# Batches in every eighth row of a quadrant, in a decode block of attention and MLP on one core

## The chip, the core and the metric

The kernel runs on one core of a Trainium2 chip. A core has a matrix engine (TensorE, PE in the profile; its weight loads are listed apart as PEld), a vector engine (VectorE, DVE), a scalar engine (ScalarE, ACT), GpSimd (POOL) and SyncE (SP), which here only issues DMAs. The engines run beside each other and wait for one another on semaphores. Sixteen DMA engines move data between the chip's memory (HBM) and the core's on-chip memory (SBUF, 128 partitions); TensorE writes into a second one (PSUM, 128 partitions). Compute engines read both, DMAs here only HBM and SBUF.

The metric is the time of one execution on the device, in microseconds (us). The kernel before takes 214.59 us, the median of three runs (214.48 to 214.62).

## The reference

One decode step for a batch of four tokens. `x` has 448 numbers per token; there are 16 query heads on 8 key and value heads, of 256 numbers each. Attention sees the last 1024 of 4096 cached positions. Everything is float32.

```python
h  = x + attention(layernorm(x), k_cache, v_cache, wq, wo)     # window W = 1024
y  = layernorm(layernorm(h))
h2 = h + gelu(y @ w1 + b1) @ w2 + b2                           # 448 -> 1792 -> 448
```

The caches dominate: per key/value head, 4 batches x 1024 positions x 256 numbers for the keys and as much for the values, read once.

## The kernel before, in words

**Quadrants.** A matmul with few output rows uses only a part of the matrix engine. The kernel therefore gives each group of 32 output partitions (a quadrant) a matmul of its own, four beside each other. In the attention one quadrant is one batch. From the attention's output projection on, one quadrant `j` holds one quarter of the columns, and the four batches are rows `32 j + 0, 1, 2, 3` of it: the first four rows of each quadrant. The other 28 rows hold zeros or are not used. `Q` is 32, `B` is 4, `P` is 128, `H` is 64, `D` is 448, `F` is 1792, `FQ` is 448 (a quarter of `F`).

**Loads.** All large loads are issued by SP in program order through `load` (line 52): `wq0`, then `k0`, two small pieces `wq1_last` (line 73), and then keys and values of the heads in turn (`k1`, `v0`, `k2`, `v1`, ...), some 5 MB each, with the projection's weights packed behind them. Keys and values have a ring of two buffers each. The last loads are the values of head 7 in four pieces, `w1` in two and `w2` in three (8, 4 and 2 of its 14 chunks). The framework gives the DMAs, SP's and ACT's in one count, eight semaphores in turn; a DMA that gets a semaphore again first waits for the one that had it before.

**The small rows.** `rs` (lines 129 to 133) is a tile of 128 x 704: a quarter of `x`, of `b2` and of `b1` for each quadrant, in its first four rows. POOL clears it, then ACT issues four DMAs, one for a quadrant, each of 4 rows of 2816 bytes. It is read first on line 358, when the attention is done.

**The heads.** Each head's round projects the next queries, makes scores (line 182), softmax, transposes (207), values (219), normalises (236), transposes the output (240) and copies it into `oT` (lines 243 and 244): a tile of 128 x 4 x 32, cleared once at the start, of whose 32 columns the first four are written. `add_output` (248) multiplies it with `wo` into `acc`; its stationary operand is the whole 32 columns, so that a quadrant's other 28 rows come out zero. The last head's product (line 335) goes straight into four quadrants, 112 or 128 columns each.

**The end of the kernel.** Line 358 adds `x` and sums; two row means over the quadrants (line 349) centre the rows; `pz` (373) turns the rows into columns with `rows_of`, the columns of the identity that stand for the batches, as the moving operand; line 374 copies them into `zT`. Line 388 multiplies `zT` with `w1`, four chunks by four quadrants, into `pu`: the first chunk with 32 stationary columns, the other three with the 4 that hold batches. Line 401 scales and adds `b1`, 402 is gelu, lines 407 and 409 transpose with `rows_of` into `put`, lines 411 (DVE) and 414 (ACT) copy into `gT`. Line 421 multiplies the first 8 chunks of `gT` with `w2` into `pa` (chunks 0 to 3 with 32 columns, 4 to 7 with 4), ACT copies `pa` to `pas` (425). Line 431 multiplies chunks 8 to 13 into `py`, the first of them with 32 columns and the others with 4; after chunk 9 line 256 adds `pas`. Line 437 adds `hb` (residual and `b2`) into `res`, and line 438 stores `res`, all 128 partitions of 128 numbers. The host picks the first four rows of each quadrant.

The order of TensorE's work is the program's, written out by hand, with a few idle matmuls (`keep_warm`, line 308) between; the other engines' order is set by the framework's scheduler.

Of the kernel before, what the change touches and what calls it, by code (L numbers as in the profile page):

```python
# [8 lines left out]
F32 = mybir.dt.float32  # L9
# [6 lines left out]
B, D = 4, 448  # L16
HQ, HKV, SK, DH = 16, 8, 4096, 256
REP = HQ // HKV
W = min(4096, max(256, SK // 4))
F = 1792  # L20
P = 128
H = P // 2
ND = 4
NKC = W // P
NFC = F // P
FQ = F // 4
Q = 32
CACHE = NKC * B * DH
WEIGHTS = 4 * D
EPS = 1e-5  # L30
# [3 lines left out]
def block_kernel(ctx: ExitStack, tc, rows, wq0, k0, wq1, kq, vo, w1, w2, out):  # L34
    nc = tc.nc
# [12 lines left out]
    def load(kind, src, pieces, name):  # L48
        t = ring.tile([P, CACHE + WEIGHTS], F32, tag=kind, name=name)
        at = 0  # L50
        for n in pieces:
            nc.sync.dma_start(t[:, at : at + n], src[:, at : at + n])  # L52
            at += n
        return t


    def wq_parts(t, last=None):
        parts = [(a, yT[:, a, :], slice(0, 512), t[:, a * 512 : (a + 1) * 512]) for a in range(3)]
        if last is not None:
            return parts + [(3, yT[:H, 3, :], slice(0, 512), last)]  # L60
        for i in range(2):
            parts.append((3, yT[:, 3 + i, :], slice(i * 2 * P, (i + 1) * 2 * P), t[:, 3 * 512 :]))
        return parts


    def load_k(g):
        half = CACHE // 2
        if g == 0:
            t = load("k", k0, (CACHE + 3 * 512,), "k0")


            for i in range(2):
                nc.sync.dma_start(
                    wq1_last[i * Q : (i + 1) * Q, :], wq1[i].rearrange("e (p c) -> e p c", c=512)[:, :4, :]
                )
            last = wq1_last
        else:
            pieces = (CACHE + WEIGHTS,) if g + 1 < HKV else (CACHE,)
            t = load("k", kq[g - 1], pieces, f"k{g}")
            last = None  # L80
        kt = [t[:, i * half : (i + 1) * half].rearrange("p (c b k) -> p c b k", c=2, b=B) for i in range(2)]
        return kt, wq_parts(t[:, CACHE:], last) if g + 1 < HKV else None


    def load_v(g):
        pieces = (CACHE + WEIGHTS,)
        if g == HKV - 1:
            pieces = (CACHE // 4, CACHE // 2, CACHE // 4, WEIGHTS)
        t = load("v", vo[g], pieces, f"v{g}")
        v = t[:, :CACHE].rearrange("p (c b d) -> p c b d", c=NKC, b=B)  # L90
        return [v[:, c : c + 2] for c in range(0, NKC, 2)], t[:, CACHE:].rearrange("p (j e) -> p j e", j=4)


    ident = const.tile([P, P], F32, name="ident")
# [5 lines left out]

    sel = const.tile([P, Q], F32, name="sel")
    nc.vector.tensor_add(sel, ident[:, 0:Q], ident[:, Q : 2 * Q])
    nc.vector.tensor_add(sel, sel, ident[:, 2 * Q : 3 * Q])
    nc.vector.tensor_add(sel, sel, ident[:, 3 * Q : 4 * Q])


    yT = const.tile([P, ND + 1, Q], F32, name="yT")
    nc.vector.memset(yT, 0.0)
    wq1_last = const.tile([H, 512], F32, name="wq1_last")
    zT = const.tile([P, ND, Q], F32, name="zT")  # L110
# [5 lines left out]
        nc.vector.tensor_scalar_mul(fold[: 3 * Q, j, :], sel[: 3 * Q, :], 1.0 / D)  # L116
        nc.vector.tensor_scalar_mul(fold[3 * Q :, j, :], sel[3 * Q :, :], 0.5 / D)
    fold = fold.rearrange("p j q -> p (j q)")
    rows_of = ident.rearrange("p (j q) -> p j q", j=4)[:, :, :B]
    qT = [const.tile([P, 2, B, Q], F32, name=f"qT{i}") for i in range(2)]  # L120
    pT = [const.tile([P, NKC // 2, B, Q], F32, name=f"pT{i}") for i in range(2)]
    oT = [const.tile([P, 4, Q], F32, name=f"oT{i}") for i in range(2)]
    gT = const.tile([P, NFC, Q], F32, name="gT")
# [4 lines left out]

    rs = const.tile([P, 2 * P + FQ], F32, name="rs")
    nc.gpsimd.memset(rs, 0.0)  # L130
    for j in range(4):
        nc.scalar.dma_start(rs[j * Q : j * Q + B, :], rows[j])
    xb, b2b, b1b = rs[:, :P], rs[:, P : 2 * P], rs[:, 2 * P :]


# [14 lines left out]
    def rsqrt(dst, var, name):  # L150
        ve = work.tile(list(dst.shape), F32, tag="ve", name=f"ve_{name}")
        nc.vector.tensor_scalar_add(ve, var, EPS)  # L152
        nc.gpsimd.tensor_tensor(dst, ve, mhalf[: dst.shape[0], : dst.shape[1]], op=ALU.pow)  # L153
# [74 lines left out]
    def columns(t, j):  # L228
        if j < 3:
            return t[:, j * P : (j + 1) * P].rearrange("p (i c) -> p i c", i=2)  # L230
        return t[:, None, 3 * P :].to_broadcast([t.shape[0], 2, H])


    def transposed_output(g, po, rec):
        o = work.tile([P, 2, DH], F32, tag="o", name=f"o{g}")
        nc.vector.tensor_scalar_mul(o, po, rec)  # L236
        pt = ps_m.tile([P, 2, 2, P], F32, tag="m", name=f"pot{g}")
        for i in range(2):
            for c in range(2):
                nc.tensor.transpose(pt[:, i, c], o[:, i, c * P : (c + 1) * P], ident)  # L240
        dst = oT[g % 2].rearrange("p (r c) q -> p c r q", r=REP)[:, :, :, :B]
        src = pt.rearrange("p i c (b q) -> p i c q b", b=B)
        nc.vector.tensor_copy(dst, src[:, 0, :, :REP])  # L243
        nc.vector.tensor_add(dst, dst, src[:, 1, :, REP : 2 * REP])  # L244
# [9 lines left out]
    def add_quadrants(dst, t, start):  # L254
        for j in range(4):
            nc.tensor.matmul(dst[j * Q : (j + 1) * Q], sel, columns(t, j), start=start, stop=False)  # L256
# [20 lines left out]
    p, rec = scores(0, kt)  # L277
    project_q(1, wqt)
    transpose_p(0, p)
    for g in range(HKV - 2):  # L280
        kt, wqt = load_k(g + 1)
        vt, wot = load_v(g)
        p, rec_next = scores(g + 1, kt)
# [9 lines left out]
    g = HKV - 2  # L293
# [6 lines left out]
    w2t = [t[:, c * D : (c + 1) * D] for c in range(NFC)]  # L300
    p, rec_last = scores(g + 1, kt)
# [4 lines left out]
    def keep_warm(n, warm):  # L306
        for _ in range(n):
            nc.tensor.matmul(warm[:Q], idle[:, :Q], idle, start=True, stop=True)  # L308
# [24 lines left out]
    for i in range(4):  # L333
        for j in range(4):
            nc.tensor.matmul(
                ph[j * Q : (j + 1) * Q], oT[(g + 1) % 2][:, i, :], columns(wo_last[:, i, :], j),
                start=False, stop=(i == 3),
# [3 lines left out]
    def w1_part(a, j):  # L341
        if a < 3:
            return slice(0, P), w1t[a][:, FQ * j : FQ * (j + 1)]
        rows = slice(H * (j // 2), H * (j // 2) + H)
        return rows, w1t[a][rows, FQ * (j % 2) : FQ * (j % 2 + 1)]


    def row_mean(sums, at, name):
        nc.tensor.matmul(at, fold, sums, start=True, stop=True)
        return at  # L350

    def stat(name):
        return once.tile([P, 1], F32, tag=name, name=name)
# [6 lines left out]
    m = row_mean(hs, pm[:, 0:1], "m")  # L360
# [4 lines left out]
    m = row_mean(ds, pm2[:, 0:1], "m2")  # L365
# [5 lines left out]
    nc.scalar.activation(junk, z, AF.Square, accum_out=zv)  # L371
    pz = ps_m.tile([P, 4, B], F32, tag="m", name="pz")
    nc.tensor.matmul(pz, z, rows_of, start=True, stop=True)
    nc.vector.tensor_copy(zT[:, :, :B], pz)
    hb = once.tile([P, P], F32, tag="hb", name="hb")
    nc.vector.tensor_add(hb, h, b2b)
    keep_warm(1, warm)
# [4 lines left out]
    pu = ps_s.tile([P, 512], F32, tag="s", name="pu")[:, :FQ]  # L382
    pv = ps_m.tile([P, 2], F32, tag="m", name="pv")
    for a in range(ND):
        m = Q if a == 0 else B
        for j in range(4):
            rows, w = w1_part(a, j)
            nc.tensor.matmul(
                pu[j * Q : j * Q + m, :], zT[rows, a, :m], w, start=(a == 0), stop=(a == ND - 1),
            )  # L390
        if a == 0:
            rsqrt(r1, row_mean(dv, pv[:, 0:1], "v1"), "r1")
        if a == 1:
            v2 = stat("v2")
            nc.vector.tensor_scalar(v2, row_mean(zv, pv[:, 1:2], "v2"), r1, r1, op0=ALU.mult, op1=ALU.mult)
            rsqrt(s, v2, "r2")
            nc.vector.tensor_mul(s, s, r1)
# [7 lines left out]
    put = ps_m.tile([P, 4, 4, B], F32, tag="m", name="put")  # L405
# [2 lines left out]
    for rows in (slice(0, H), slice(H, P)):  # L408
        nc.tensor.matmul(put[rows, 3], u[:, 3 * P :], rows_of, start=True, stop=True)
    dst = gT[:, :12, :].rearrange("p (c j) q -> p c j q", c=3)  # L410
    nc.vector.tensor_copy(dst[:, :, :, :B], put[:, :3])

    for i, rows in enumerate((slice(0, H), slice(H, P))):
        nc.scalar.copy(gT[rows, 12:, :B], put[rows, 3].rearrange("p (j i) q -> p j i q", i=2)[:, :, i, :])
    keep_warm(1, warm)

    first = 8
    pa = ps_w.tile([P, D], F32, tag="acc", name="pa")
    for c in range(first):
        j, m = c % 4, Q if c < 4 else B  # L420
        nc.tensor.matmul(
            pa[j * Q : j * Q + m, :], gT[:, c, :m], w2t[c], start=(c < 4), stop=(c >= first - 4),
        )
    pas = once.tile([P, D], F32, tag="u", name="pas")
    nc.scalar.copy(pas, pa)
    py = ps_o.tile([P, 2, H], F32, tag="o", name="py")
    for c in range(first, NFC):
        for j in range(4):
            m, n = (Q, 2) if c == first else (B, 2 if j < 3 else 1)
            w = columns(w2t[c], j) if n == 2 else w2t[c][:, None, 3 * P :]  # L430
            nc.tensor.matmul(  # L431
                py[j * Q : j * Q + m, :n, :], gT[:, c, :m], w, start=(c == first), stop=(c == NFC - 1),
            )
        if c == first + 1:
            add_quadrants(py, pas, False)
    res = once.tile([P, P], F32, tag="res", name="res")
    nc.vector.tensor_add(res, py.rearrange("p i c -> p (i c)"), hb)  # L437
    nc.sync.dma_start(out, res)


# [64 lines left out]
```

## Time and profile before

| | before |
|---|---|
| median of 3 runs | 214.59 us (214.48 to 214.62) |
| profiled execution, from first to last instruction (span) | 212.9 us |
| TensorE busy | 137.9 us (65%) |
| VectorE busy | 39.2 us (18%) |
| ScalarE busy | 21.0 us (10%) |
| GpSimd busy | 5.6 us (3%) |
| DMA moved | 88.46 MB, 415 GB/s over the span |
| mean granted TensorE clock | 0.872 |

The profile is of one execution and prints no other time of it than its span; the runs above are others. The median of the runs is 1.7 us above the span. Busy time is an instruction's own time; waits are not in it. The page's second part cuts the span into 40 slices, its fourth follows the chain of work that ended last back from the last instruction. Matmuls of float32 appear twice in the lists, since each runs in two passes.

### The profile page before, as it was taken

What the parts mean: (1) busy time and instruction counts of PE and PEld (TensorE: products, weight loads), DVE (VectorE), ACT (ScalarE), POOL (GpSimd) and SP (SyncE); (2) the same over time, 40 slices, a digit from 0 to 9 for tenths busy, and PEclk for the clock granted to TensorE, in tenths of its full rate; (3) what the DMA queues carried; (4) which work ended last, traced back from release to release, by engine and by line L of the source; (5) the groups of instructions that cost most, each with busy time, mean ns of one, the idle gap of its engine ahead of it and who ended that gap; (6) DMA issues with size and microseconds to landing.
All of it is one profiled execution on the core that took longest, in us unless ns stands there. A gap on an engine that the chain in (4) does not pass through costs nothing.

```text
span 212.9 us, 2306 instructions
## 1 busy us (share of the span) xinstructions
PE 137.9 (65%) x971; PEld 49.1 (23%) x971; DVE 39.2 (18%) x167; ACT 21.0 (10%) x52; POOL 5.6 (3%) x17
## 2 busy tenths in 40 slices
PE   0456868093886739583986348382948476798994
PEld 0322233021231212211231113120222123234432
DVE  1420324001130202210130104110230231022320
ACT  0210213000030000300030003000030001000311
POOL 6100000000000000000000000000000000000110
PEclk9999999669597966969599859979797999699999
DMA  7999998999989999999999999999989999999991
GB/s 291 426 399 469 398 465 378 459 465 390 458 378 465 465 390 458 398 446 465 390 458 405 443 465 386 465 413 428 461 375 468 440 428 390 417 418 433 424 390 60
DMA packets 3865, 88.46 MB, mean 415 GB/s; under 512 B 448, under 2 KB 576, under 8 KB 1168
## 3 DMA queue, kind: packets, MB, share of 16 engines
q1 hardware_dynamic: 3824, 88.29, 96.9%
q8 instruction: 7, 0.11, 0.2%
q10 hardware_dynamic: 32, 0.05, 0.1%
q14 instruction: 2, 0.02, 0.0%
HBM read 88.26 MB, written 0.07 MB: 415 GB/s over the span
## 4 chain that ended last, share of the span: by engine, by line
DMA 85%; PE 11%; DVE 2%; issue 0%; SPq 0%
DMA v<-vo 65%; DMA w<-w 12%; DMA k<-k 8%; PE po L219 8%; PE acc L248 1%; DVE o L236 1%; PE pot L240 1%; PE py L431 1%; DVE oT L243 0%; DVE oT L244 0%; SPq L52 0%; DVE res L437 0%; PE py L256 0%
## 5 line engine op out<-in xcount | busy, mean ns | idle before, releaser
L182 PE MATMUL s<-k,qT 128*32 128x512 f32 x256 | 42.3, 822 | 24.7 <-DMA k<-kq 22.6
L219 PE MATMUL po<-v,pT 128*32 128x512 f32 x256 | 40.0, 772 | 19.6 <-DMA v<-vo 19.6
L186 DVE TENSOR_REDUCE mx<-s 128x1 f32<-128x512 f32 x16 | 11.1, 691 | 67.4 <-PE s L182 67.4
L182 PEld LDWEIGHTS s<-k,qT 128*32 128x32 f32 x256 | 10.0, 146 | 54.7 <-issue 29.4
L219 PEld LDWEIGHTS po<-v,pT 128*32 128x32 f32 x256 | 10.7, 135 | 42.3 <-issue 31.4
L161 ACT COPY qs<-pq 128x512 f32<-128x512 f32 x8 | 4.7, 586 | 135.8 <-PE pq L159 135.8
L236 DVE TENSOR_SCALAR o<-po,rec 128x512 f32<-128x512 f32 x8 | 6.0, 750 | 60.2 <-PE po L219 60.2
L194 ACT ACTIVATE p<-s,nm 128x512 f32<-128x512 f32 x16 | 10.9, 690 | 18.4 <-DVE nm L190 18.4
L207 PE MATMUL ppt<-ident,p 128*128 128x128 f32 x64 | 10.5, 286 | 2.0 <-ACT p L194 1.7
L165 PE MATMUL pqt<-ident,qs 128*128 128x128 f32 x32 | 5.7, 304 | 6.2 <-ACT qs L161 6.2
L240 PE MATMUL pot<-ident,o 128*128 128x128 f32 x32 | 5.2, 286 | 5.7 <-DVE o L236 5.7
L248 PE MATMUL acc<-v,oT 128*32 128x448 f32 x56 | 6.7, 551 | 3.3 <-DVE oT L244 3.3
L207 PEld LDWEIGHTS ppt<-ident,p 128*128 128x128 f32 x64 | 6.7, 140 | 6.0 <-ACT p L194 6.0
L159 PE MATMUL pq<-k,yT 128*32 128x512 f32 (+1 forms) x66 | 7.3, 515 | 0.0
L308 PE MATMUL warm<-idle 128*32 128x512 bf16 x25 | 7.3, 382 | 0.0
L240 PEld LDWEIGHTS pot<-ident,o 128*128 128x128 f32 x32 | 3.3, 140 | 13.0 <-DVE o L236 13.0
L165 PEld LDWEIGHTS pqt<-ident,qs 128*128 128x128 f32 x32 | 3.6, 150 | 10.9 <-ACT qs L161 9.1
L153 POOL TENSOR_TENSOR r<-ve_r,mhalf 128x1 f32<-128x1 f32 x2 | 1.1, 544 | 191.9 <-DVE ve_r L152 191.9
L211 DVE COPY pT<-ppt 128x16 f32<-128x16 f32 x32 | 4.7, 170 | 4.7 <-PE ppt L207 4.7
L159 PEld LDWEIGHTS pq<-k,yT 128*32 128x32 f32 x66 | 3.1, 110 | 6.1 <-issue 4.8
L138 PE MATMUL pm_x<-wq,mean 128*128 128x12 f32 x2 | 0.6, 363 | 5.8 <-DMA wq<-wq 5.8
L167 DVE TENSOR_REDUCE sm<-pqt 128x16 f32<-128x64 f32 x8 | 1.8, 225 | 13.0 <-PE pqt L165 13.0
(101 smaller groups left out, 60.9 us busy)
## 6 DMA issues: line engine op xcount, KB each, us to landing
v<-vo SPq DMA_DIRECT2D x7, 4992.0 KB, 31.8
k<-kq SPq DMA_DIRECT2D x6, 4992.0 KB, 32.0
k<-k SPq DMA_DIRECT2D x1, 4864.0 KB, 16.3
k<-kq SPq DMA_DIRECT2D x1, 4096.0 KB
w<-w SPq DMA_DIRECT2D x2, 1792.0 KB
v<-vo SPq DMA_DIRECT2D x2, 1024.0 KB, 22.2
v<-vo SPq DMA_DIRECT2D x1, 2048.0 KB
w<-w SPq DMA_DIRECT2D x1, 1344.0 KB
```

The lines of the kernel that those rows point to most:

```text
L159: nc.tensor.matmul(pq[j * Q : (j + 1) * Q, cols], y, w, start=True, stop=True)
L161: nc.scalar.copy(qs, pq)
L165: nc.tensor.transpose(pt[:, i, :], qs[:, i * P : (i + 1) * P], ident)
L182: nc.tensor.matmul(s[b * Q : (b + 1) * Q, :], qT[g % 2][:, c, b, :], kt[h][:, c, b, :], start=(c == 0), stop=(c == 1),)
L186: nc.vector.reduce_max(mx[:, h : h + 1], s, axis=AX.X)
L194: nc.scalar.activation(p[:, h * 512 : (h + 1) * 512], halves[h], AF.Exp, bias=nm, scale=SCALE, accum_out=sums[:, h : h + 1],)
L207: nc.tensor.transpose(pt[:, c, :], p[:, (4 * h + c) * P : (4 * h + c + 1) * P], ident)
L219: nc.tensor.matmul(po[b * Q : (b + 1) * Q], pT[g % 2][:, c, b, :], vt[c][:, :, b, :], start=(c == 0), stop=(c == NKC // 2 - 1),)
L236: nc.vector.tensor_scalar_mul(o, po, rec)
L240: nc.tensor.transpose(pt[:, i, c], o[:, i, c * P : (c + 1) * P], ident)
L248: nc.tensor.matmul(acc[i * Q : (i + 1) * Q, :], oT[g % 2][:, i, :], wt[:, i, :], start=(g == 0), stop=(g == HKV - 2),)
L308: nc.tensor.matmul(warm[:Q], idle[:, :Q], idle, start=True, stop=True)
```

## The change

The four batches of a quadrant move from rows 0, 1, 2, 3 to rows 0, 8, 16, 24, from the attention's output on. All sixteen rows of a tile are then one pattern, every eighth of the 128 partitions. With it:

- `rows_of` takes every eighth column of the identity; `oT`, `zT` and `gT` are written in every eighth column.
- `rs` comes by one DMA of 16 rows on partitions 0, 8, ..., 120; the host hands `rows` over as 16 x 704.
- The matmuls of lines 388, 421 and 431 take all 32 columns of the stationary operand in every chunk. Before, all but the first took 4.
- The store takes every eighth partition of `res`: 16 rows of 128 numbers, and the output tensor is 16 x 128 instead of 128 x 128.

Nothing else is edited; the instructions of TensorE, VectorE, ScalarE and GpSimd stand in the same order, but for three DMA issues fewer on ACT. With three DMAs fewer the turn of the eight semaphores moves on: `k1` and `v0` wait for none at their issue after it.

```diff
+STEP = Q // B
...
-    rows_of = ident.rearrange("p (j q) -> p j q", j=4)[:, :, :B]
+    rows_of = ident.rearrange("p (j q) -> p j q", j=4)[:, :, ::STEP]
...
-    for j in range(4):
-        nc.scalar.dma_start(rs[j * Q : j * Q + B, :], rows[j])
+    nc.scalar.dma_start(rs[::STEP, :], rows)
...
-        dst = oT[g % 2].rearrange("p (r c) q -> p c r q", r=REP)[:, :, :, :B]
+        dst = oT[g % 2].rearrange("p (r c) q -> p c r q", r=REP)[:, :, :, ::STEP]
...
-    nc.vector.tensor_copy(zT[:, :, :B], pz)
+    nc.vector.tensor_copy(zT[:, :, ::STEP], pz)
...
     for a in range(ND):
-        m = Q if a == 0 else B
...
-                pu[j * Q : j * Q + m, :], zT[rows, a, :m], w, start=(a == 0), stop=(a == ND - 1),
+                pu[j * Q : (j + 1) * Q, :], zT[rows, a, :], w, start=(a == 0), stop=(a == ND - 1),
...
-    nc.vector.tensor_copy(dst[:, :, :, :B], put[:, :3])
+    nc.vector.tensor_copy(dst[:, :, :, ::STEP], put[:, :3])
...
-        nc.scalar.copy(gT[rows, 12:, :B], put[rows, 3].rearrange("p (j i) q -> p j i q", i=2)[:, :, i, :])
+        nc.scalar.copy(gT[rows, 12:, ::STEP], put[rows, 3].rearrange("p (j i) q -> p j i q", i=2)[:, :, i, :])
...
-        j, m = c % 4, Q if c < 4 else B
+        j = c % 4
         nc.tensor.matmul(
-            pa[j * Q : j * Q + m, :], gT[:, c, :m], w2t[c], start=(c < 4), stop=(c >= first - 4),
+            pa[j * Q : (j + 1) * Q, :], gT[:, c, :], w2t[c], start=(c < 4), stop=(c >= first - 4),
...
-            m, n = (Q, 2) if c == first else (B, 2 if j < 3 else 1)
+            n = 2 if c == first or j < 3 else 1
...
-                py[j * Q : j * Q + m, :n, :], gT[:, c, :m], w, start=(c == first), stop=(c == NFC - 1),
+                py[j * Q : (j + 1) * Q, :n, :], gT[:, c, :], w, start=(c == first), stop=(c == NFC - 1),
...
-    nc.sync.dma_start(out, res)
+    nc.sync.dma_start(out, res[::STEP, :])
...
+    rows = rows.reshape(4 * B, 2 * P + FQ)
...
-    out = nc.dram_tensor("out", (P, P), F32, kind="ExternalOutput").ap()
+    out = nc.dram_tensor("out", (4 * B, P), F32, kind="ExternalOutput").ap()
```

More of the change, by code (lines that the diff above doesn't have):

```diff
@@ L502 @@
     r = run(nc, [arrays], core_ids=[0])
-    got = np.asarray(r.results[0]["out"]).reshape(4, Q, P)[:, :B, :]
+    got = np.asarray(r.results[0]["out"]).reshape(4, B, P)
     return np.ascontiguousarray(got.transpose(1, 0, 2).reshape(B, 1, 4 * P)[:, :, :D])
```

## The prediction

> **What bounds the kernel now.** I read the page's DMA rows first, since the slices of DMA are at 9 nearly throughout.
>
> ```profile
> span 212.9 us, 2306 instructions
> ...
> DMA  7999998999989999999999999999989999999991
> ...
> q1 hardware_dynamic: 3824, 88.29, 96.9%
> q8 instruction: 7, 0.11, 0.2%
> q10 hardware_dynamic: 32, 0.05, 0.1%
> ```
>
> The bulk queue q1 keeps 16 DMA engines at 96.9% of the span. One engine moves 88.29 MB / (0.969 x 16 x 212.9 us) = 26.7 KB in a microsecond. Stretches of time (span, busy time of the engines, granted clock, DMA share, GB/s) show how full this is and how it ends:
>
> ```profile
> 17.00:42.00 25.00, 16.08 (x106) 6.05 (x106) 5.74 (x26) 3.87 (x10) 0.00 (x0) 0.94 1.01 435
> ...
> 90.00:140.00 50.00, 32.03 (x216) 10.01 (x212) 7.92 (x32) 3.87 (x10) 0.00 (x0) 0.81 1.01 433
> ...
> 206.00:207.00 1.00, 0.90 (x9) 0.32 (x12) 0.17 (x1) 0.32 (x2) 0.00 (x0) 1.00 0.97 398
> 207.00:208.00 1.00, 1.00 (x12) 0.13 (x4) 0.00 (x0) 0.00 (x0) 0.00 (x0) 1.00 0.68 276
> 208.00:209.00 1.00, 0.63 (x27) 0.59 (x28) 0.00 (x0) 0.53 (x1) 0.00 (x0) 1.00 0.39 154
> ```
>
> The DMA engines have no gap (a share of 1 in the middle), so no wait of the heads, and no earlier issue of a load, moves the end: the stream ends when its bytes are through. It ends raggedly: about a third of the engines are idle between 207 and 208, two thirds after 208. A load is complete when its slowest engine is, so the slowest engine sets the end. The end of the chain of waits (start, duration, what):
>
> ```profile
> 182.14 26.22 DMA w<-w
> ...
> 208.41 0.64 PE py L431 x13
> 209.05 0.17 PE py L256 x6
> 209.22 0.97 PE py L431 x19
> ...
> 210.21 0.29 DVE res L437
> ```
>
> So: stream to 208.4, 1.8 us of last matmuls, the addition, the store. What is off this path until then costs nothing.
>
> **The store.** The issue, the stretches behind it, and the wait for it:
>
> ```profile
> 210.53 0.35 SPq L438 DMA_DIRECT2D out<-res  x1
> ```
> ```profile
> 210.50:211.30 0.80, 0.00 (x0) 0.00 (x0) 0.01 (x1) 0.00 (x0) 0.00 (x0) 1.00 0.00 0
> 211.30:211.40 0.10, 0.00 (x0) 0.00 (x0) 0.00 (x0) 0.00 (x0) 0.00 (x0) 1.00 0.11 31
> 211.40:211.50 0.10, 0.00 (x0) 0.00 (x0) 0.00 (x0) 0.00 (x0) 0.00 (x0) 1.00 0.75 225
> 211.50:211.60 0.10, 0.00 (x0) 0.00 (x0) 0.00 (x0) 0.00 (x0) 0.00 (x0) 1.00 0.98 287
> 211.60:211.70 0.10, 0.00 (x0) 0.00 (x0) 0.00 (x0) 0.00 (x0) 0.00 (x0) 1.00 0.39 108
> 211.70:211.80 0.10, 0.00 (x0) 0.00 (x0) 0.00 (x0) 0.00 (x0) 0.00 (x0) 1.00 0.03 5
> 211.80:212.90 1.10, 0.00 (x0) 0.00 (x0) 0.00 (x0) 0.00 (x0) 0.00 (x0) 1.00 0.00 0
> ```
>
> Nothing else runs then, so every nanosecond saved here counts. The shares sum to 2.26 x 0.10 = 0.226 us of busy time for each engine: 8 of the 128 rows each, 0.028 us a row. With 16 rows an engine has one: 7 x 0.028 = 0.20 us go. The engines also start and end apart (0.11 first, 0.03 last), some of which goes with the seven rows: I take 0.22. Bounds: 0, if what follows the packets does not depend on their number, and 0.40, if the whole busy stretch from 211.3 shrinks to one slice. The time from issue to first packet (about 0.8 us) and from last packet to the end (1.1) I leave as they are: no row shows them for a smaller store. The Trainium skill's page "DMA: Bandwidth & Descriptors" (section "Anatomy of one DMA") gives a DMA a fixed 2.0 us plus its bytes at 436 GB/s; by that 56 KB less would be an estimated 0.13 us, and the sum below 0.09 higher; the trace's 0.226 us of packets for 64 KB is more than that formula's 0.15, so I stay with the row.
>
> **The rows of x and biases.** Bytes are the same (16 x 2816 B = 45 KB) but they sit on other engines. The q10 row has 32 packets for four transfers of four rows: 16 rows, and 16 more, one completion mark for each row's engine, four in a transfer. So a transfer of four rows runs on four engines. On one engine a row takes 2.816 / 26.7 = 0.105 us of the full stream. The new transfer gives each of the 16 engines one row. The engine that ends last had between 0 and 4 of the old rows, so the end moves by +0.105 to -0.32 us. No view prints engines; I followed the packets of the trace end to start, and the engine that ended last seems to be one that carried no row, so I take +0.10. The same skill page (section "Why a DMA increments its semaphore by 16 and not by 1") says that such a transfer uses the lowest-numbered engines; the trace agrees on four of them, and shows no numbers.
>
> A later end of the stream counts in full: `pa` waits for the first piece of `w2`, `py` for the second. An earlier one does not, because of the other input of line 256:
>
> ```profile
> 206.33 1.71 PE L421 MATMUL pa<-w,gT 128*32 128x448 f32 x16
> ...
> 208.15 0.53 ACT L425 COPY pas<-pa 128x448 f32<-128x448 f32 x1 [1.62 <-PE pa L421]
> ...
> 208.78 0.48 PE L256 MATMUL py<-pas,sel 128*32 128x128 f32 x8
> ```
>
> `pas` is ready at 208.68 and its matmuls start at 208.78: the most that an earlier `w2` can bring is 0.10 us, then `pas` is late.
>
> Three issues fewer on ACT:
>
> ```profile
> 4.07 1.54 ACTq L132 DMA_DIRECT2D rs<-rows  x4
> ...
> 13.62 0.59 ACT L161 COPY qs<-pq 128x512 f32<-128x512 f32 x1 [6.69 <-PE pq L159]
> ```
>
> ACT's next work waits 6.7 us for the matmuls anyway: 0. The rows themselves are first read 190 us later. `k1` and `v0` are issued earlier, into a queue that is full: 0. SP's later loads wait for buffers as before.
>
> **Wider stationary operands.** Rows by form (busy, mean ns):
>
> ```profile
> L388 PE MATMUL pu<-w,zT 128*4 128x448 f32 x16 | 1.9, 539 | 0.0
> ...
> L431 PEld LDWEIGHTS py<-w,gT 128*4 128x4 f32 x40 | 1.1, 86 | 0.1
> ...
> L388 PE MATMUL pu<-w,zT 128*32 128x448 f32 x8 | 1.0, 551 | 0.0
> ...
> L256 PE MATMUL py<-pas,sel 128*32 128x128 f32 x8 | 0.5, 273 | 0.0
> ...
> L411 DVE COPY gT<-put 128x48 f32<-128x48 f32 x1 | 0.2, 208 | 1.3 <-PE put L409 1.3
> ...
> L256 PEld LDWEIGHTS py<-pas,sel 128*32 128x32 f32 x8 | 0.2, 110 | 0.0
> ...
> L374 DVE COPY zT<-pz 128x16 f32<-128x16 f32 x1 | 0.2, 175 | 0.5 <-PE pz L373 0.5
> ```
>
> A load of 32 columns takes 110 ns, of 4 columns 86: 24 more. Four quadrants load beside each other, so it counts once a pass: `pu` 3 chunks, `pa` 1 group of four, `py` 5 chunks, two passes each, 18 passes. Fully exposed that is 18 x 24 = 0.43 us; hidden, 0. Loads overlap the matmuls before them. Those of `pu` and `pa` take 540 ns, far above a load. Those of `py` are short, but line 256 has 32 columns now, its matmuls take the same 273 ns, and its eight end in 0.48 us, so a pass there starts about 0.48 - 0.27 = 0.21 us after the pass before it at most. I take 0.02 us for ten passes in `py`.
>
> **Strided copies and columns.** `zT` and `gT` are written, and `rows_of` read, at a step of eight numbers. The rows have no such step; 16 to 48 numbers differ by 208 - 175 = 33 ns for 32, 1 ns each, so even twice the price is 16 + 48 ns on the path, and the same kind of copy already jumps between groups of four. I take 0, with 0.06 as the upper end and nothing below. `oT` (lines 243, 244) lies in the heads, under the full stream: 0; for head 7 it is under the wait for `w2`.
>
> **Sum.** +0.10 (rows) + 0.02 (weights) - 0.22 (store) = -0.10 us: a span of 212.8 where the profile has 212.9. The page prints no other time of this execution; the median of the runs, 214.59, is 1.7 above the span, and I carry the difference over: 214.49 us.
>
> **Rivals.**
> 1. The stream ends earlier, because the last engine is one of the four. For: they carried four rows each, 0.42 us. Against: my reading of the packets. Price: 0.10 at most, by `pas`, instead of +0.10: 214.59 - 0.10 + 0.02 - 0.22 = 214.29. With a store at its upper end (0.40) 214.11. Chance 0.22, about half of it beyond 0.43 us of gain.
> 2. Slower: one engine gets two instruction loads. The q8 row has 7 packets of 16 KB, 0.2% of 16 x 212.9 us = 6.8 us, 0.97 each: an engine that takes one is behind by that, and the ragged end is of this size. If the moved rows and semaphores let the last engine take another, the end comes 0.97 later: 214.49 + 0.97 = 215.46. It decides as soon as that engine is among the last ones already. Against: TensorE's instructions stay the same in number and order. Chance 0.09.
> 3. The weight loads show. For: `py` is short and at the very end. Against: line 256. 214.59 + 0.10 + 0.43 - 0.22 = 214.90. Chance 0.11, a third of it beyond 0.43 with strided copies dear as well.
> 4. The store doesn't get shorter, as what follows the packets sets it: 214.59 + 0.12 = 214.71. Chance 0.10.
>
> **How the numbers follow.** The forecast has 0.48. What a measurement can tell from no change is about 0.2%, 0.43 us, and the forecast is well inside. Faster: half of rival 1 and a little for a store that starts sooner, 0.15. Slower: rival 2, a third of rival 3, 0.13. Within: 0.72. The range leaves out rival 2 and the ends of 1 and 3: 214.10 to 214.95.
>
> **What would show it.** Right: in the last stretch the DMA share after the store's issue lies in two slices of 0.1 us with a sum near 0.03 us, and issue to end falls from 2.4 to about 2.15; `w2` releases `py` about 0.1 later than 208.37; matmuls of 32 columns in `py` at 273 ns, the chain from the first `py` to `res` 1.8 us; q10 with 32 packets again. Wrong: `py` released before 208.3 (rival 1) or past 209 (2), more than 1.9 us of `py` (3), the same 2.4 us after the issue (4).

## The result, and the profile after

The changed kernel takes 215.17 us (215.10 to 215.47), the kernel before beside it 214.48 (214.38 to 214.62): a ratio of 1.0033, 95% interval 1.0022 to 1.0043. It is slower by 0.69 us, where 0.10 less was forecast. The spans of its executions are 213.3 to 213.7 us, their median 213.4; those of the kernel before, 31 executions measured later, have a median of 212.7.

The page of the changed kernel:

```profile
span 213.3 us, 2302 instructions
...
DMA  7999899998999989999999999999999998999980
...
q1 hardware_dynamic: 3712, 88.23, 96.6%
q8 instruction: 7, 0.11, 0.2%
q10 hardware_dynamic: 32, 0.05, 0.1%
```

The stream is as full as before, q10 has 32 packets again, q1 has 112 fewer (the store's rows). The chain of waits ends like this (start, duration, what):

```profile
181.96 26.39 DMA w<-w
...
208.40 0.64 PE py L430 x13
209.04 0.17 PE py L256 x6
209.21 0.97 PE py L430 x19
...
210.20 0.29 DVE res L436
```

In this execution the stream releases `py` at 208.40, as in the profile of before (208.41), and the last product takes the same 1.80 us. All of the time by which this pair of profiles differs lies behind the start of line 436: the kernel before ended 2.7 us after the start of `res` (212.9 - 210.21), this one 3.1 (213.3 - 210.20). First the issue of the store, then stretches of 0.1 us behind it (the DMA share is the number before the last):

```profile
210.52 0.59 SPq L437 DMA_DIRECT2D out<-res  x1
```
```profile
211.30:211.40 0.10, 0.00 (x0) 0.00 (x0) 0.00 (x0) 0.00 (x0) 0.00 (x0) 1.00 0.00 0
...
211.60:211.70 0.10, 0.00 (x0) 0.00 (x0) 0.00 (x0) 0.00 (x0) 0.00 (x0) 1.00 0.00 0
211.70:211.80 0.10, 0.00 (x0) 0.00 (x0) 0.00 (x0) 0.00 (x0) 0.00 (x0) 1.00 0.16 36
211.80:211.90 0.10, 0.00 (x0) 0.00 (x0) 0.00 (x0) 0.00 (x0) 0.00 (x0) 1.00 0.23 41
```

The packets are indeed fewer: shares of 0.16 and 0.23, 0.04 us for an engine where 0.226 were. But SP's issue takes 0.59 us instead of 0.35, and the first packet comes 1.24 us after it instead of 0.84 (by the packet records). What is saved at the packets is lost twice over ahead of them: the last one ends 0.2 us later.

A second loss is on SP, behind the landing. Line 499 is the program's end: SP makes five waits there one after the other, each for two semaphores (the eight of the DMAs are among them), and then drains. Its rows before the change, and after it:

```profile
L499 SPq EVENT_SEMAPHORE  x7: 17/28/28, 210.9 to 212.9; - x7
...
L499 SPq DRAIN  x3: 7/7/13, 212.2 to 212.5; - x3
```
```profile
L499 SPq EVENT_SEMAPHORE  x7: 17/28/28, 211.2 to 213.2; - x7
...
L499 SPq DRAIN  x3: 7/7/7, 212.6 to 212.9; - x3
```

Single waits can be read from the records of the trace. Before the change the store was the 32nd DMA and had the semaphore that is waited for last; the other four waits were over before it landed (they start at 210.93, 211.00, 211.06 and 211.13, the fifth ends at 212.13). Now it is the 29th of 29, and its semaphore is in the second wait. That wait ends at 212.34, and three waits at a distance of 0.06 us follow, to 212.53. That is 0.19 us.

So 0.2 + 0.19 us are in the profiles. The rest of the 0.69 is not in this pair, since the profile of before was of an execution with a span above its median (212.9 against 212.7). The experiments look for it in the medians.

### The profile page after: what moved, and what is told of

It is laid out like the page before. It is cut to its first block, busy times and chain, and to the rows that moved or that the text cites. A ratio compares the mean times of both kernels' runs of the same rounds, so it can differ in the third digit from the quotient of the medians.

```text
span 213.3 us, 2302 instructions
## 1 busy us (share of the span) xinstructions
PE 132.0 (62%) x971; PEld 47.3 (22%) x971; DVE 39.4 (18%) x167; ACT 21.0 (10%) x52; POOL 5.6 (3%) x17
## 4 chain that ended last, share of the span: by engine, by line
DMA 85%; PE 9%; DVE 2%; SPq 1%; issue 1%
DMA v<-vo 73%; DMA w<-w 12%; PE po L219 6%; PE acc L248 1%; DVE o L236 1%; PE pot L240 1%; PE py L430 1%; SPq L74 1%; SPq L53 1%; DVE oT L243 0%; DVE oT L244 0%; DVE res L436 0%; PE py L256 0%
## 5 line engine op out<-in xcount | busy, mean ns | idle before, releaser
L219 PE MATMUL po<-v,pT 128*32 128x512 f32 x256 | 33.2, 662 | 21.1 <-DMA v<-vo 21.0
L219 PEld LDWEIGHTS po<-v,pT 128*32 128x32 f32 x256 | 8.6, 119 | 40.0 <-issue 25.6
```

The lines of the kernel that those rows point to most:

```text
L219: nc.tensor.matmul(po[b * Q : (b + 1) * Q], pT[g % 2][:, c, b, :], vt[c][:, :, b, :], start=(c == 0), stop=(c == NKC // 2 - 1),)
```

## The experiments

All are compared with the kernel before, run on the same chip; "ahead" and "behind" are meant from the start of `res`.

**The kernel before, against itself.**

> The kernel before, against itself: it gives the span of each of its executions, which the first page had for one alone, and the noise of the comparison. Both theories: 214.5 us, ratio 1.000 within 0.001, spans of 212.7 to 212.9.

214.51 us, ratio 0.9997 (0.9989 to 1.0006), spans of 212.6 to 212.8. Its profile has `py` at 208.16, 0.25 earlier than the first one: the end of the stream differs by that from one execution to another, so one profile of each kernel cannot tell a quarter of a microsecond ahead of `res`, and I use medians there and profiles behind it.

**The store of 128 rows back.**

```diff
-    nc.sync.dma_start(out, res[::STEP, :])
+    nc.sync.dma_start(out, res)
```

> The changed kernel with the store of all 128 rows as before; one load of the 16 rows is kept. Theory (the loss is at the very end: the 16-row store starts its packets 0.40 us later and saves 0.19 of them, net +0.21; and three more waits stand behind the store's, +0.19, because three DMAs fewer move the store to another semaphore): the store's first packet comes back to 0.85 us after its issue, the three waits stay, so about 0.2 us of the 0.69 go: 214.9 to 215.0. Rival (the one load on sixteen engines makes the stream longer, 0.3 us): the store gives back 0.2 here too, but what is left stands ahead of the store, at the release of py. Rival (wider stationary operands): the time from the first py to res is over 1.8 us.

214.89 us, ratio 1.0019 (1.0010 to 1.0028). The issue is short again:

```profile
208.38 0.64 PE py L430 x13
...
210.19 0.29 DVE res L436
```
```profile
210.51 0.35 SPq L437 DMA_DIRECT2D out<-res  x1
```

It ends at 213.1, 2.9 us after the start of `res`: between the 2.7 of before and the 3.1 of the change. The difference of 0.18 to the kernel before, with the same store, is the three waits. The rest of what is left in the medians (214.89 against 214.53 for the kernel before beside it) stands ahead of `res`.

**Four loads of rows back.**

```diff
-    nc.scalar.dma_start(rs[::STEP, :], rows)
+    for j in range(4):
+        nc.scalar.dma_start(rs[j * Q : (j + 1) * Q : STEP, :], rows[j * B : (j + 1) * B, :])
```

> The changed kernel with four loads of 4 rows (every eighth partition of a quadrant) in place of one; the 16-row store is kept. The store gets the last semaphore again, as before the change, and the rows sit on four engines. Theory: the three waits behind the store's go, 0.19 us, and whatever the stream lost by the one load; the store's late packets stay: 214.7, +0.2 on the kernel before. Rival (the load on sixteen engines costs 0.3 in the stream): the same 214.7, but then py is released about 0.2 to 0.3 us earlier than in the changed kernel's median execution. If the waits cost nothing: 214.9.

214.92 us, ratio 1.0021 (1.0011 to 1.0031), 0.2 above what I expected. Its tail is as expected (`res` at 210.52, end at 213.4: 2.9 us, the store alone). But the part ahead did not come back with the four loads. These four are spaced, as the one load of the change is; those of the kernel before are not.

**Both transfers back**, the store of 128 rows and the four loads, which stay on every eighth partition.

> The changed kernel with both transfers undone (four loads, store of 128 rows); what is left of the change is the stride in the compute instructions and the 32 stationary columns. Theory: 214.5, the kernel before within 0.1%. Rival (wider stationary operands or strided copies cost): 214.7 or more, with py to res above 1.8 us or pas ready after 208.7.

214.78 us, ratio 1.0011 (1.0002 to 1.0019). Behind `res` nothing is left (210.14 to 212.8: 2.7 us), and `py` to `res` is 1.80 us. Still 0.25 us are lost, all ahead of `py`. It can be the stationary columns, or the loads, whose spacing is not undone here.

**Wide stationary operands alone**, in the kernel before:

```diff
-        m = Q if a == 0 else B
+        m = Q
...
-        j, m = c % 4, Q if c < 4 else B
+        j, m = c % 4, Q
...
-            m, n = (Q, 2) if c == first else (B, 2 if j < 3 else 1)
+            m, n = Q, 2 if c == first or j < 3 else 1
```

> The kernel before with 32 stationary columns in every chunk of the last three products, and nothing else changed. The kernel with both transfers undone still lost 0.25 us (ratio 1.0011), with the same 1.80 us from py to res. Theory (width costs nothing): 214.5, spans of 212.7. Rival (width is what is left): 214.75, spans of 213.0.

214.58 us, ratio 1.0004 (0.9995 to 1.0013): nothing that this can tell from zero. In the changed kernel's rows by form (busy, mean ns) the wide operands and the spaced copies read so:

```profile
L430 PE MATMUL py<-w,gT 128*32 128x128 f32 x38 | 1.7, 275 | 0.4 <-DMA w<-w 0.4
L430 PEld LDWEIGHTS py<-w,gT 128*32 128x32 f32 x48 | 1.3, 109 | 1.2 <-DMA w<-w 1.2
...
L410 DVE COPY gT<-put 128x48 f32<-128x48 f32 x1 | 0.2, 244 | 1.3 <-PE put L408 1.3
...
L374 DVE COPY zT<-pz 128x16 f32<-128x16 f32 x1 | 0.2, 185 | 0.5 <-PE pz L373 0.5
```

The loads take 109 ns beside matmuls of 275. The spaced copies do cost something (244 ns instead of 208, 185 instead of 175), ahead of a wait for `w2`.

**Spaced row loads alone**, in the kernel before:

```diff
-        nc.scalar.dma_start(rs[j * Q : j * Q + B, :], rows[j])
+        nc.scalar.dma_start(rs[j * Q : (j + 1) * Q : Q // B, :], rows[j])
```

> The kernel before with its four row loads put on every eighth partition of a quadrant, and nothing else changed (the rest still reads rows 0 to 3 of a quadrant, so x and biases reach one batch alone and the output is not the block's). Theory (what is left of the loss with both transfers undone comes from where the loads of rows put them): 214.75, spans of 213.0, and the first packets of k1 slow on all engines between 16 and 17.6 us, as in the two kernels with four loads of every eighth row. Rival (it does not): 214.5, spans of 212.7.

214.79 us, ratio 1.0010 (1.0001 to 1.0019): 0.27 between the medians, as much as the whole remainder of the kernel with both transfers undone (0.25). ACT's issues, and the next thing it does:

```profile
4.07 3.02 ACTq L132 DMA_DIRECT2D rs<-rows  x4
7.12 1.28 ACT L161 ACT_TABLE_LOAD   x1 [7.12 <-issue]
```

Four issues take 3.02 us where the adjacent rows took 1.54. The four one by one (shortest, median and longest in ns), in the kernel before and here:

```profile
L132 ACTq DMA_DIRECT2D rs<-rows x4: 260/316/557, 4.1 to 5.3; - x4
```
```profile
L132 ACTq DMA_DIRECT2D rs<-rows x4: 583/589/1173, 4.1 to 6.5; - x4
```

The packet records also show twelve of the first packets of `k1`, near 16.5 us, that take 69 to 115 ns more than the usual 1.48 us; in the kernel before one alone is longer by so much (by 445). How the one leads to the other, and to 0.25 us at the end, these runs don't show.

**Neighbouring rows in the store.** Same number of rows, no spacing:

```diff
-    nc.sync.dma_start(out, res[::STEP, :])
+    nc.sync.dma_start(out, res[: 4 * B, :])
```

> The changed kernel, but the store takes the first 16 partitions of res, which are neighbours, and not every eighth (the result is then not the block's output). It tells the number of rows from their spacing. Theory (the spacing makes SP's issue long, 0.59 us instead of 0.35, and the first packet late): the issue takes 0.35 us again and the first packet comes 0.84 us after it. Rival (a transfer whose row count differs from that of the loads before it takes longer to issue): 0.59 us and 1.24 us stay.

The issue and the DMA shares behind it:

```profile
210.25 0.29 DVE L436 TENSOR_TENSOR res<-py,hb 128x128 f32<-128x128 f32 x1 [3.96 <-PE py L430]
210.57 0.36 SPq L437 DMA_DIRECT2D out<-res  x1
```
```profile
211.30:211.40 0.10, 0.00 (x0) 0.00 (x0) 0.00 (x0) 0.00 (x0) 0.00 (x0) 1.00 0.00 0
211.40:211.50 0.10, 0.00 (x0) 0.00 (x0) 0.00 (x0) 0.00 (x0) 0.00 (x0) 1.00 0.24 51
211.50:211.60 0.10, 0.00 (x0) 0.00 (x0) 0.00 (x0) 0.00 (x0) 0.00 (x0) 1.00 0.17 31
211.60:211.70 0.10, 0.00 (x0) 0.00 (x0) 0.00 (x0) 0.00 (x0) 0.00 (x0) 1.00 0.00 0
```

The one execution took 214.76 us. The issue takes 0.36 us, and the packets come 0.85 us after its start. The end comes 2.72 us after the start of `res`, with the three waits behind it: 0.15 less than the 128 rows with the same waits (2.88), and 0.39 less than the same 16 rows spaced (3.11). So fewer rows do save, and the spacing costs more than they save.

**The store in two halves.**

```diff
-    nc.sync.dma_start(out, res[::STEP, :])
+    for i in range(2):
+        nc.sync.dma_start(out[i * 2 * B : (i + 1) * 2 * B, :], res[i * H : (i + 1) * H : STEP, :])
```

> The changed kernel with its store cut into two of 8 rows, every eighth partition each, back to back on SP. If the long issue is the price of the pattern each time, both take about 0.59 us, and the end comes 0.6 us later than in the changed kernel. If it is the price of the first transfer of another shape after many of 128 rows, the second takes 0.26 to 0.35 us, like the second to fourth load of rows on ACT in the kernel before (0.26, 0.31, 0.32 after a first of 0.56).

```profile
210.67 1.28 SPq L438 DMA_DIRECT2D out<-res  x2
```

The two issues take 0.64 and 0.59 us: the price is paid each time and is not that of a first transfer of another shape. The one execution took 215.80 us, 0.6 above the changed kernel, as expected for two long issues.

**The waits behind the store**, with the changed kernel run again as the mark:

```diff
     nc.scalar.dma_start(rs[::STEP, :], rows)
+    tiny = const.tile([1, 3], F32, name="tiny")
+    for i in range(3):
+        nc.scalar.dma_start(tiny[:, i : i + 1], rows[i : i + 1, :1])
```

> The changed kernel once more, as the mark for the other three on the same chip: 215.1 to 215.2 us, spans of 213.4.

> The changed kernel with three more loads of 4 bytes each on ACT at the start, which nothing reads: as many DMAs as the kernel before, so the store gets the last of the eight semaphores and no wait stands behind its own. Theory (the three waits cost 0.19 us): 0.19 us less than the changed kernel, 214.95, and drain 0.06 us after the store's wait. Rival (the waits are hidden, the loss is in the transfers alone): 215.15 as the changed kernel, or more by three more DMAs.

215.18 us (ratio 1.0029, 1.0018 to 1.0040) for the changed kernel again, and 215.07 (1.0026, 1.0015 to 1.0036) with three useless loads more. The end of the latter:

```profile
L502 SPq EVENT_SEMAPHORE  x7: 17/28/28, 211.2 to 213.1; - x7
...
L502 SPq DRAIN  x3: 7/7/13, 212.4 to 212.7; - x3
```

The store is issued 0.06 us later than in the changed kernel (210.58) and SP drains 0.2 us earlier (212.4 for 212.6). `res` to end is 2.92 us for 3.11: 0.19, as expected. Of it 0.11 is left in the medians, whose intervals overlap; the profile carries this verdict, not the medians. All kept profiles agree on it. From the start of `res` to the end they take 2.70 to 2.71 us with 128 rows on the last semaphore (six profiles), 2.88 with 128 rows and three waits behind, 2.89 to 2.93 with 16 spaced rows on the last semaphore (five), and 3.11 with 16 spaced rows and three waits behind (two).

**No row loads at all**, in both kernels (four loads of 4 bytes in their place, so that the store keeps the last semaphore):

> The kernel before without its four row loads, four loads of 4 bytes in their place (x in the residual and both biases are then zero, and the output is not the block's); the count of DMAs is kept. If the engine that ends last carries none of the rows, as I read it: 214.5, as the kernel before. If it carries them: down to 214.1.

> The changed kernel without its row load, four loads of 4 bytes in its place (x in the residual and both biases zero, the output not the block's); the store is on the last semaphore. Theory (ahead of the store, the changed kernel loses 0.1 to 0.3 us by the row that each engine carries): this one and the kernel before without rows reach res at the same time, and it ends 0.2 later by the store alone: 214.7. Rival (what is lost ahead of the store is not the rows): it ends 0.4 to 0.5 us after the kernel before without rows.

214.58 us (ratio 1.0000, 0.9991 to 1.0009) and 214.81 (1.0012, 1.0003 to 1.0020). In the kernel before the loads cost nothing at the end that this can tell. The time alone could not refute an ending engine with rows, since `pas` lets an earlier `w2` bring 0.10 us at most; but `py` is released at 208.20 without the rows and at 208.16 and 208.41 in the two profiles with them, where four rows fewer on that engine would be 0.42 earlier. In the changed kernel, with the same semaphore for the store, the one load costs 215.07 - 214.81 = 0.26 us. Without rows the two kernels' chains agree; the kernel before without rows,

```profile
208.20 0.64 PE py L432 x13
...
210.01 0.29 DVE res L438
```

and the changed one without:

```profile
208.14 0.64 PE py L432 x13
...
209.94 0.29 DVE res L438
```

They reach `res` within 0.07 us of each other, and the changed one ends 0.23 us later: that is the store alone, without waits and without rows.

**What the row load's price goes by.** 0.26 is more than the 0.105 of its bytes. The load cut to 512 bytes a row:

```diff
-    nc.scalar.dma_start(rs[::STEP, :], rows)
+    nc.scalar.dma_start(rs[::STEP, :P], rows[:, :P])
```

> The changed kernel with three loads of 4 bytes more, and its row load cut to the 128 columns of x: 512 bytes a row instead of 2816 (the biases stay zero, so the output is not the block's). The row load of 2816 bytes cost 0.26 us ahead of the store (215.07 against 214.81 without it), where its bytes on an engine are 0.105. If the cost goes by bytes it falls to 0.05: 214.86. If most of it is a fixed price for a second queue's packet and its mark among the first one's, 0.15 and a little stay: 214.98.

214.77 us (ratio 1.0011, 1.0002 to 1.0020): not above the kernel without rows (214.81, on another chip, with 214.56 and 214.54 for the kernels before). The profile here is of the slowest of eleven executions (214.94) and has `res` at 210.24, as late as with whole rows, so this rests on the medians. And the load issued by SP behind `k0`, in the bulk's own queue:

```diff
-    nc.scalar.dma_start(rs[::STEP, :], rows)
...
     kt, wqt = load_k(0)
+    nc.sync.dma_start(rs[::STEP, :], rows)
```

> The changed kernel with three loads of 4 bytes more, and its row load issued by SP behind k0 and wq1_last, in the queue of the bulk, instead of by ACT in a queue of its own. If the price above 0.105 us is that of two queues on an engine, it goes: 214.91. If it is not, 215.07 stay.

215.03 us (ratio 1.0021, 1.0012 to 1.0030): 0.22 above no rows. So by the medians the price falls with the bytes, and it is not that of a second queue. Why it is about twice what the bytes take on one engine stays open; the intervals of the single ratios are 0.2 us to either side, so that 0.105 is not excluded by them. Nor is it shown that the price comes from a row on every engine. Four spaced loads cost the kernel before 0.27 us on as few engines as its four neighbouring ones, which cost nothing that the medians show, so the spacing may be part of the 0.26 as well. One load of the 16 whole rows to neighbouring partitions would tell the two apart, and was not run.

No kernel tried here is faster than the one before by more than the noise. Sixteen neighbouring rows would save 0.15 us at the store, but the quadrants start at partitions 0, 32, 64 and 96, so the batches of all four are not neighbours.

## Why the prediction was wrong

The parts as measured: the store +0.23, three waits behind it +0.19, the row load +0.26, the width 0: 0.68 of the 0.62 to 0.69. The 0.19 is read from profiles; the medians of one chip, from the changed kernel back to the one before, give 0.11 for the waits, 0.26 for the row load, 0.23 for the store and 0.02 for the rows of before, 0.62 in all.

**What bounds the kernel**: right. The stream is full in every run, releases `py`, and everything behind it is serial. That is why 0.2 us at the very end show in full. Only "stream to 208.4" is loosely read: what lands there is the second piece of `w2`, and packets of the third run on to 208.98, which no matmul waits for.

**The store, -0.22: the step that failed.** I priced the packets and left "the time from issue to first packet ... as they are", since no row showed it for a smaller store. The packets went nearly as worked out (0.04 us of busy time for an engine instead of 0.226, 0.18 less), and with neighbouring rows the store does save 0.15 us. But spaced rows put the first packet 0.40 us later, so that the store cost 0.23 us where 0.22 less was forecast. The Trainium skill's page "DMA: Bandwidth & Descriptors" (section "Anatomy of one DMA") fits its 2.0 us plus bytes at 436 GB/s to transfers issued from GpSimd, while this store is issued by SP. By the term of the bytes alone the saving would be an estimated 0.13 us, near the 0.15 measured with neighbouring rows. The fit has no term for where the rows lie. My range for the store ended at 0 because I saw no way that a smaller store could cost more, and I varied only its size. The change alters two things of the store, its size and its pattern, and the second had no row in the trace of before, so it should have been bounded from both sides. A hint stood in that trace: SP's two loads of `wq1_last`, the only ones on SP with another pattern than 128 neighbouring rows, took 0.82 and 0.68 us to issue, and every plain one 0.33 to 0.43.

```profile
1.18 0.41 SPq L52 DMA_DIRECT2D k<-k  x1
1.63 1.55 SPq L73 DMA_DIRECT2D wq_last<-wq  x2
```

**The semaphores, 0**: failed. I followed the turn of the semaphores through the loads, where it costs nothing, and not to the end of the program, where the order of the last waits gives the store's semaphore a price. The 1.1 us "from last packet to the end" that I left as they are contained it: 0.19 more now.

**The rows of x and biases, +0.10**: the sign was right, the size too small, and the mechanism is not shown. That the engine that ends last carried no row is borne out: without its row loads the kernel before is the same (1.0000) and releases `py` no earlier. The new load costs 0.26, or 0.22 in the bulk's queue, and about 0 with 512 bytes. My upper end, 0.105, was the engine's rate alone, and by the medians too low; the spacing of the rows, for which I had no term here either, costs 0.27 in the kernel before.

**Wider stationary operands, +0.02**: right within what can be told (1.0004), and `py` to `res` kept its 1.80 us.

**Strided copies, 0 at the end**: right as far as the runs can tell (without rows the changed kernel reaches `res` no later than the one before), with 36 and 10 ns more for `gT` and `zT`, inside the 0.06 us given.

**The rivals.** Rival 4, a store that does not get shorter, pointed the right way and was too small, 214.71: it is worse than not shorter. Rival 2, a second instruction load on the last engine, would have cost 0.97 and shows nowhere. Rival 3 fell with the run of the width alone. Rival 1 fell with the kernel without rows, by its release of `py`.

## What to carry to other kernels

The lead of the last store before its first packet went by its pattern here (0.84 us with 128 neighbouring rows, 0.85 with 16, 1.24 with 16 spaced ones), not by its bytes. When the rows of a store change place, price the issue and the lead, and try the store by itself before the layout is built around it. Where semaphores are given out in turn, count the transfers up to the last one, since the last store's place among the final waits was worth 0.19 us. And where one slowest engine ends a full stream, ask of a small load which engines it uses and how its rows are spaced: here four loads of neighbouring rows on four engines cost nothing that could be told, and one spaced load of the same bytes on all sixteen 0.26 us.

## What the runs showed that I had not expected

- A DMA between SBUF and HBM can take longer to issue when its rows are spaced: 0.59 us for 16 rows at every eighth partition against 0.36 for 16 neighbours, each time and not only the first. On ACT, 4 such rows take 0.58 against 0.26 to 0.32, where another transfer went ahead. The load of 16 spaced rows took 0.56 us there as the first transfer, as long as the first of 4 neighbouring rows (0.56); but it also took 0.55 as the fourth, behind the three loads of 4 bytes.
- Four loads of 4 spaced rows cost the kernel before 0.27 us by the medians (ratio 1.0010, 1.0001 to 1.0019) ahead of a stream's end some 190 us later, at the same bytes on the same number of engines, while leaving the neighbouring ones out gains nothing. How it gets there stays open.
- Three loads of 4 bytes that nobody reads took 0.19 us off the last stretch of the changed kernel, by moving a semaphore.
